# Keeping one more chunk of the input on chip: parking it in PSUM, with the re-read order adapted

## The chip, the cores and the metric

The kernel runs on one core of a Trainium2 chip. The metric is the device time of one execution in microseconds. Times are quoted as medians of several runs, all of which agreed within about 0.6%; no run of this study was in a slow state. The span that a profile page gives is about 2 us shorter than the time of the run that it was taken from.

In the lines of the profile, PE is TensorE (PEld its weight loads), DVE is VectorE, ACT is ScalarE, POOL is GpSimd and SP is SyncE; a q behind the name (ACTq, SPq) marks work of that engine's queue, here the issue of DMA transfers. SBUF is the on-chip memory that holds this kernel's buffers for chunks of the input, here called slots; PSUM is the on-chip memory into which its matmuls write their sums.

## The reference

A squeeze-and-excitation block. All of the input has to be seen before any of the output can be made:

```python
# x: (1, 256, 256, 384) bf16, w_down: (384, 24), w_up: (24, 384)
def reference(x, w_down, w_up):
    s = x.mean(axis=(1, 2))                       # over all 65,536 pixels
    s = _sigmoid(_silu(s @ w_down) @ w_up)        # 384 gates
    return x * s[:, None, None, :]
```

The input is 50.33 MB and so is the output. At least 100.66 MB must be moved; what is not kept on chip between the mean and the multiply is read a second time.

## The kernel before

The pixels are spread over 128 partitions, 512 rows of 384 channels in each. Sixteen rows make a chunk (12,288 bytes per partition, 1.57 MB in all), so there are 32 chunks. SBUF holds 17 slots of that size. The first 15 chunks are streamed through slots only for their sums, the other 17 stay:

```python
    JS = min(J, max(1, 12288 // (C * 2)))                    # 16 rows
    chunks = [(j0, min(JS, J - j0)) for j0 in range(0, J, JS)]
    NCH = len(chunks)                                        # 32
    ...
    n_slots = max(1, min(NCH, (avail - small_bytes) // bytes_per_slot))   # 17
    NS = NCH - n_slots                                       # 15 are read twice
    ...
    p1_order = [(stream_ids[k], k % n_slots) for k in range(NS)] + [
        (cache_ids[i], i) for i in range(n_slots)
    ]
    # load phase: for each chunk one DMA load; TensorE adds the rows up,
    # 16 matmuls with a column of ones per chunk, into one PSUM bank (sums_ps)
    ...
    # mean -> two tiny matmuls -> gate [128, 384] bf16
    ...
    for i in range(n_slots):                                 # kept chunks
        if i == 0:
            scale_and_store(i, cache_ids[i], piece_rows=[1, 3, 4, 8])
        elif i == 1:
            scale_and_store(i, cache_ids[i], piece_rows=[8, 8])
        else:
            scale_and_store(i, cache_ids[i])
    for k in range(NS):                                      # re-read chunks
        sl = k % n_slots
        j0, jsz = chunks[stream_ids[k]]
        nc.sync.dma_start(out=slots[sl][:, :jsz, :], in_=x3[:, j0:j0 + jsz, :])
        scale_and_store(sl, stream_ids[k])
```

`scale_and_store` multiplies in place on VectorE (`tensor_tensor`, slot times broadcast gate) and stores from the ScalarE queue. A reload of slot k must wait until the store out of slot k has landed. Both queues' transfers use eight completion semaphores in turn (in the trace, eight numbers that come back with every eighth load), so a transfer also waits for the one eight places before it.

## Time and profile before

| | before |
|---|---|
| time, median | 308.12 us (308.00 to 308.35, 12 runs) |
| span of the profile | 306.3 us |
| bytes moved | 124.38 MB: 32 + 15 chunks read, 32 written |
| busy: TensorE / VectorE | 30% / 35% |

Head of the page of the kernel before. The GB/s row has 40 equal slices of the span; the load phase is the left part, the store phase the right one.

```profile
span 306.3 us, 1307 instructions
PE 91.1 (30%) x519; PEld 43.9 (14%) x519; DVE 106.6 (35%) x40; ACT 2.1 (1%) x4; POOL 2.5 (1%) x8
...
GB/s 294 423 424 427 422 428 425 426 424 428 424 424 427 425 428 335 50 337 390 430 428 427 430 435 428 427 426 437 430 425 428 437 427 428 428 437 425 430 428 287
DMA packets 12518, 124.38 MB, mean 406 GB/s; under 512 B 1492, under 2 KB 1632, under 8 KB 2784
...
HBM read 73.96 MB, written 50.33 MB: 406 GB/s over the span
```

No compute engine is near full. Apart from both ends and a dip in the middle, every slice stands at 422 to 437 GB/s. The windows view of the same kernel puts numbers to the stretches. Its columns are: from and to, length, then busy us (and instructions) of each engine, then the granted TensorE clock, the busy share of the DMA engines (a packet is counted whole in the stretch in which it starts, so the share can come out a little above 1), and GB/s.

```profile
4.00:119.00 115.00, 85.01 (x480) 40.81 (x480) 0.00 (x0) 0.00 (x0) 0.00 (x0) 1.00 1.01 424
119.00:131.00 12.00, 6.13 (x39) 3.02 (x38) 4.51 (x7) 0.65 (x2) 0.00 (x0) 0.89 0.35 133
131.00:143.00 12.00, 0.00 (x0) 0.00 (x0) 12.00 (x6) 0.00 (x0) 0.00 (x0) 0.50 0.97 351
143.00:302.00 159.00, 0.00 (x0) 0.00 (x0) 90.03 (x28) 0.00 (x0) 0.00 (x0) 0.50 1.01 430
```

In two stretches, 274 us together, the DMA share is 1.01 and the rate 424 to 430 GB/s: a byte less there is time less. Two lines of the timeline of the store phase (start, length, what, count, idle before) tell how far the stores run behind VectorE:

```profile
127.93 148.52 ACTq L217 DMA_DIRECT2D out_dram<-slot  x36
...
250.87 3.36 DVE L211 TENSOR_TENSOR slot<-slot,gate 128x6144 bf16<-128x6144 bf16 x1 [3.98 <-DMA slot<-in_x_dram]
```

The last multiply ends at 254.2 us, but the span ends at 306.3: 52 us of stores are queued behind it. This suggests that VectorE could be late in the store phase at no cost.

### The profile page before, as it was taken

What the parts mean: (1) busy time and instruction counts of PE and PEld (TensorE: products, weight loads), DVE (VectorE), ACT (ScalarE), POOL (GpSimd) and SP (SyncE); (2) the same over time, 40 slices, a digit from 0 to 9 for tenths busy, and PEclk for the clock granted to TensorE, in tenths of its full rate; (3) what the DMA queues carried; (4) which work ended last, traced back from release to release, by engine and by line L of the source; (5) the groups of instructions that cost most, each with busy time, mean ns of one, the idle gap of its engine ahead of it and who ended that gap; (6) DMA issues with size and microseconds to landing.
All of it is one profiled execution on the core that took longest, in us unless ns stands there. A gap on an engine that the chain in (4) does not pass through costs nothing.

```text
span 306.3 us, 1307 instructions
## 1 busy us (share of the span) xinstructions
PE 91.1 (30%) x519; PEld 43.9 (14%) x519; DVE 106.6 (35%) x40; ACT 2.1 (1%) x4; POOL 2.5 (1%) x8
## 2 busy tenths in 40 slices
PE   0977677777777777300000000000000000000000
PEld 0433233333333333100000000000000000000000
DVE  0000000000000000499999999998444442000000
ACT  1000000000000000000000000000000000000000
POOL 3000000000000000000000000000000000000000
PEclk9999999999999999855555555555555555555555
DMA  7999999999999998199999999999999999999996
GB/s 294 423 424 427 422 428 425 426 424 428 424 424 427 425 428 335 50 337 390 430 428 427 430 435 428 427 426 437 430 425 428 437 427 428 428 437 425 430 428 287
DMA packets 12518, 124.38 MB, mean 406 GB/s; under 512 B 1492, under 2 KB 1632, under 8 KB 2784
## 3 DMA queue, kind: packets, MB, share of 16 engines
q1 hardware_dynamic: 7200, 73.93, 57.7%
q10 hardware_dynamic: 5184, 50.33, 38.8%
q8 instruction: 4, 0.07, 0.1%
q0 software_dynamic: 128, 0.04, 0.1%
q14 instruction: 2, 0.02, 0.0%
HBM read 73.96 MB, written 50.33 MB: 406 GB/s over the span
## 4 chain that ended last, share of the span: by engine, by line
DMA 70%; DVE 7%; issue 2%; PE 2%; SPq 1%; ACT 0%; DVEq 0%; ACTq 0%
DMA slot<-in_x_dram 43%; DMA out_dram<-slot 28%; DVE slot L211 7%; PE sums_ps L111 2%; SPq L104 1%; DVE mean_bf L133 0%; ACT gate L189 0%; DVE z1bc L171 0%; PE zz_ps L182 0%; PE meanT_ps L143 0%; PE z_ps L161 0%; DVE meanT_sb L152 0%; ACT s L169 0%; DVEq L211 0%; SPq L231 0%
## 5 line engine op out<-in xcount | busy, mean ns | idle before, releaser
L211 DVE TENSOR_TENSOR slot<-slot,gate 128x6144 bf16<-128x6144 bf16 (+4 forms) x36 | 105.5, 2994 | 22.1 <-DMA slot<-in_x_dram 21.2
L111 PE MATMUL sums_ps<-slot,ones_bf 128*1 128x384 bf16 x512 | 90.4, 332 | 34.3 <-DMA slot<-in_x_dram 34.3
L111 PEld LDWEIGHTS <-ones_bf 128*1 128x1 bf16 x512 | 43.5, 85 | 80.8 <-issue 43.2
L133 DVE TENSOR_SCALAR mean_bf<-sums_ps 1x384 bf16<-1x384 f32 x1 | 0.5, 546 | 123.9 <-PE sums_ps L111 123.9
L127 POOL DMA_DIRECT2D wd_sb<-in_w_down_dram x3 | 1.8, 604 | 0.8 <-POOLq L247 0.8
L81 ACT ACT_TABLE_LOAD x1 | 1.3, 1283 | 0.7 <-PEq L247 0.7
L169 ACT ACTIVATE s<-z_ps 24x1 f32<-24x1 f32 x1 | 0.2, 160 | 123.8 <-PE z_ps L161 123.8
L129 POOL DMA_DIRECT2D wu_sb<-in_w_up_dram x1 | 0.5, 539 | 0.0
L182 PE MATMUL zz_ps<-wu_sb,z1bc 24*128 24x384 bf16 x1 | 0.3, 331 | 0.6 <-DVE z1bc L171 0.6
L171 DVE TENSOR_SCALAR z1bc<-z_ps,s 24x128 bf16<-24x128 f32 x1 | 0.3, 339 | 0.5 <-ACT s L169 0.5
L189 ACT ACTIVATE gate<-zz_ps 128x384 bf16<-128x384 f32 x1 | 0.5, 491 | 0.8 <-PE zz_ps L182 0.8
L143 PE MATMUL meanT_ps<-ones_bf,mean_bf 1*128 1x1 bf16 x3 | 0.2, 163 | 0.6 <-DVE mean_bf L133 0.6
L78 DVE MEMSET ones_bf<- 128x8 bf16 x1 | 0.1, 65 | 0.8 <-PEq L247 0.8
L161 PE MATMUL z_ps<-meanT_sb,wd_sb 128*24 128x1 bf16 x3 | 0.2, 163 | 0.3 <-DVE meanT_sb L152 0.3
L143 PEld LDWEIGHTS <-mean_bf 1*128 1x128 bf16 x3 | 0.1, 91 | 1.0 <-DVE mean_bf L133 1.0
L152 DVE CAST meanT_sb<-meanT_ps 128x3 bf16<-128x3 f32 x1 | 0.2, 163 | 0.3 <-PE meanT_ps L143 0.3
L161 PEld LDWEIGHTS <-wd_sb 128*24 128x24 bf16 x3 | 0.2, 89 | 0.3 <-issue 0.2
L81 ACT ACTIVATE dummy<-ones_bf 1x1 f32<-1x1 bf16 x1 | 0.2, 202 | 0.0
L182 PEld LDWEIGHTS <-z1bc 24*128 24x128 bf16 x1 | 0.1, 90 | 0.7 <-DVE z1bc L171 0.7
L247 POOL MEMSET const-bfloat16-1.0<- 128x1 bf16 x1 | 0.1, 102 | 0.0
L247 POOL MEMSET const-float32-0.0<- 128x1 f32 x1 | 0.1, 99 | 0.2 <-issue 0.2
L247 POOL MEMSET const-float32-1.0<- 128x1 f32 x1 | 0.1, 99 | 0.0
(1 smaller groups left out, 0.1 us busy)
## 6 DMA issues: line engine op xcount, KB each, us to landing
slot<-in_x_dram SPq DMA_DIRECT2D x46, 1536.0 KB, 29.4
out_dram<-slot ACTq DMA_DIRECT2D x30, 1536.0 KB, 29.2
out_dram<-slot ACTq DMA_DIRECT2D x3, 768.0 KB, 3.8
slot<-in_x_dram SPq DMA_DIRECT2D x4, 384.0 KB, 22.8
out_dram<-slot ACTq DMA_DIRECT2D x1, 384.0 KB, 2.3
out_dram<-slot ACTq DMA_DIRECT2D x1, 288.0 KB, 2.1
out_dram<-slot ACTq DMA_DIRECT2D x1, 96.0 KB, 1.7
wd_sb<-in_w_down_dram POOLq DMA_DIRECT2D x3, 6.0 KB, 5.9
```

The costliest lines, as they stand in the source:

```text
L81: nc.scalar.activation(out=dummy[:1, :1], in_=ones_bf[0:1, 0:1], func=ACT.Sigmoid)
L104: nc.sync.dma_start(out=st[:, r0:r0 + rsz, :], in_=x3[:, j0 + r0:j0 + r0 + rsz, :])
L111: nc.tensor.matmul(sums_ps[ci][:1, :csz], ones_bf[:, 0:1], st[:, jj, c0:c0 + csz], start=first, stop=last,)
L127: nc.gpsimd.dma_start(out=wd_sb[:csz, kt, :], in_=w_down[c0:c0 + csz, :])
L129: nc.gpsimd.dma_start(out=wu_sb[:R, :], in_=w_up[:, :])
L133: nc.vector.tensor_scalar(out=mean_bf[:1, c0:c0 + csz], in0=sums_ps[ci][:1, :csz], scalar1=1.0 / float(N), scalar2=None, op0=ALU.mult,)
L143: nc.tensor.matmul(meanT_ps[:csz, kt:kt + 1], mean_bf[0:1, c0:c0 + csz], ones_bf[0:1, 0:1], start=True, stop=True,)
L161: nc.tensor.matmul(z1_ps[:R, 0:1], wd_sb[:csz, kt, :], meanT_sb[:csz, kt:kt + 1], start=(kt == 0), stop=(kt == KT - 1),)
L182: nc.tensor.matmul(zz_ps[:, :csz], z1bc[:R, :], wu_sb[:R, c0:c0 + csz], start=True, stop=True,)
L189: nc.scalar.activation(out=gate[:, c0:c0 + csz], in_=zz_ps[:, :csz], func=ACT.Sigmoid)
L211: nc.vector.tensor_tensor(out=st[:, r0:r0 + rsz, :], in0=st[:, r0:r0 + rsz, :], in1=gate_b, op=ALU.mult,)
L247: nc = _bacc.Bacc("TRN2", target_bir_lowering=False, num_devices=1)
```

## The change

By the constants that the program reads when it is built (`PSUM_NUM_BANKS`, `PSUM_BANK_SIZE_BYTES`), PSUM has eight banks of 2 KB per partition, and the kernel needs two at a time. The change takes the other six, exactly 12,288 bytes per partition (the tile `xps`, 128x3072 fp32), to keep one more chunk. All of the kernel's big loads and stores go to and from slots in SBUF, so VectorE copies the chunk in (as fp32 words) while its sum is taken, and later multiplies straight out of PSUM into a slot that is stored. Slot 1 serves as that staging slot, so its own reload is moved to the end. The small PSUM tiles now share banks.

```diff
+    psum_misc_banks = len(cn_chunks) + 1
+    ...
+        spare = ((psum_banks_total - psum_misc_banks) * nc.PSUM_BANK_SIZE_BYTES) // (C * 2)
+        psum_rows = max(0, min(spare, JS, J - cached_rows))          # 16
+    streamed_rows = J - cached_rows - psum_rows                      # 14 chunks
 ...
-        psum.tile([1, csz], FP32, name=f"sums_ps_{i}")
+        psum.tile([1, csz], FP32, name=f"sums_ps_{i}", tag=f"wide{i}")
+        xps = psum.tile([P, psum_rows, C // 2], FP32, name="xps")
 ...
+        def park(st):
+            nc.vector.tensor_copy(out=xps[:, :, :], in_=st[:, :pjsz, :].bitcast(FP32))
+        read_and_reduce(pj0, pjsz, psl, after=park)
 ...
-    meanT_ps = psum.tile([P, KT], FP32)
+    meanT_ps = psum.tile([P, KT], FP32, tag="narrow")
 ...  (z1_ps: tag "narrow"; zz_ps: tag "wide")
+                in0=src[:, r0:r0 + rsz, :] if src is not xps else src[:, r0:r0 + rsz, :].bitcast(BF16),
 ...
+    if psum_chunk is not None:
+        pj0, pjsz = psum_chunk
+        stage_sl = 1 if n_slots > 1 else 0
+        stage = slots[stage_sl]
+        scale_and_store(xps, stage, pj0, pjsz)
-    for k in range(NS):
-        sl = k % n_slots
-        j0, jsz = chunks[stream_ids[k]]
-        nc.sync.dma_start(out=slots[sl][:, :jsz, :], in_=x3[:, j0:j0 + jsz, :])
-        scale_and_store(sl, stream_ids[k])
+    for k in [0] + list(range(2, NS)) + [1]:
+        j0, jsz = stream_chunks[k]
+        st = slots[k % n_slots]
+        nc.sync.dma_start(out=st[:, :jsz, :], in_=x3[:, j0:j0 + jsz, :])
+        scale_and_store(st, st, j0, jsz)
```

(Cut: the bookkeeping of chunk lists and the split of the load helper, which leave the work as it is.)

More of the change, by code (lines that the diff above doesn't have):

```diff
@@ L42 @@
     JS = min(J, max(1, 12288 // (C * 2)))
-    chunks = [(j0, min(JS, J - j0)) for j0 in range(0, J, JS)]
-    NCH = len(chunks)
     bytes_per_slot = _pad32(JS * C * 2)
@@ L58 @@
     avail = nc.sbuf_top - nc.sbuf_base
-    n_slots = max(1, min(NCH, (avail - small_bytes) // bytes_per_slot))
-    NS = NCH - n_slots
-    stream_ids = list(range(NS))
-    cache_ids = list(range(NS, NCH))
+    n_slots = max(1, min((J + JS - 1) // JS, (avail - small_bytes) // bytes_per_slot))
+    cached_rows = min(J, n_slots * JS)
+    psum_banks_total = nc.PSUM_NUM_BANKS
+    psum_misc_banks = len(cn_chunks) + 1
+    psum_rows = 0
+    if J > cached_rows and psum_misc_banks < psum_banks_total:
+        spare = ((psum_banks_total - psum_misc_banks) * nc.PSUM_BANK_SIZE_BYTES) // (C * 2)
+        psum_rows = max(0, min(spare, JS, J - cached_rows))
+    streamed_rows = J - cached_rows - psum_rows
+    stream_chunks = []
+    j0 = 0
+    rem = streamed_rows % JS
+    if rem:
+        stream_chunks.append((j0, rem))
+        j0 += rem
+    while j0 < streamed_rows:
+        stream_chunks.append((j0, JS))
+        j0 += JS
+    NS = len(stream_chunks)
+    psum_chunk = (streamed_rows, psum_rows) if psum_rows > 0 else None
+    cache_chunks = []
+    j0 = streamed_rows + psum_rows
+    while j0 < J:
+        rows = min(JS, J - j0)
+        cache_chunks.append((j0, rows))
+        j0 += rows
+    assert len(cache_chunks) == n_slots or J <= cached_rows
+    n_slots = len(cache_chunks)
     x3 = x.flatten_outer_dims().rearrange("(p j) c -> p j c", p=P)
@@ L83, with reduce_rows, read_and_reduce @@
     sums_ps = [
-        psum.tile([1, csz], FP32, name=f"sums_ps_{i}")
+        psum.tile([1, csz], FP32, name=f"sums_ps_{i}", tag=f"wide{i}")
         for i, (c0, csz) in enumerate(cn_chunks)
     ]
-    p1_order = [(stream_ids[k], k % n_slots) for k in range(NS)] + [
-        (cache_ids[i], i) for i in range(n_slots)
-    ]
+    xps = None
+    if psum_chunk is not None:
+        xps = psum.tile([P, psum_rows, C // 2], FP32, name="xps")
     total_mm = J
     mm_state = {"idx": 0}
-    def read_and_reduce(ch, sl, pieces):
-        j0, jsz = chunks[ch]
+    def reduce_rows(st, r0, rsz):
+        for jj in range(r0, r0 + rsz):
+            first = mm_state["idx"] == 0
+            last = mm_state["idx"] == total_mm - 1
+            for ci, (c0, csz) in enumerate(cn_chunks):
+                nc.tensor.matmul(
+                    sums_ps[ci][:1, :csz],
+                    ones_bf[:, 0:1],
+                    st[:, jj, c0:c0 + csz],
+                    start=first,
+                    stop=last,
+                )
+            mm_state["idx"] += 1
+    def read_and_reduce(j0, jsz, sl, pieces=1, after=None):
         st = slots[sl]
@@ L106, in read_and_reduce @@
             )
-            for jj in range(r0, r0 + rsz):
-                first = mm_state["idx"] == 0
-                last = mm_state["idx"] == total_mm - 1
-                for ci, (c0, csz) in enumerate(cn_chunks):
-                    nc.tensor.matmul(
-                        sums_ps[ci][:1, :csz],
-                        ones_bf[:, 0:1],
-                        st[:, jj, c0:c0 + csz],
-                        start=first,
-                        stop=last,
-                    )
-                mm_state["idx"] += 1
-    for n, (ch, sl) in enumerate(p1_order):
-        remaining = len(p1_order) - n
-        pieces = 4 if remaining == 1 else 1
-        read_and_reduce(ch, sl, pieces)
+            reduce_rows(st, r0, rsz)
+        if after is not None:
+            after(st)
+    for k, (j0, jsz) in enumerate(stream_chunks):
+        read_and_reduce(j0, jsz, k % n_slots)
+    if psum_chunk is not None:
+        pj0, pjsz = psum_chunk
+        psl = NS % n_slots
+        def park(st):
+            nc.vector.tensor_copy(out=xps[:, :, :], in_=st[:, :pjsz, :].bitcast(FP32))
+        read_and_reduce(pj0, pjsz, psl, after=park)
+    for i, (j0, jsz) in enumerate(cache_chunks):
+        pieces = 4 if (i == n_slots - 1 and jsz >= 4) else 1
+        read_and_reduce(j0, jsz, i, pieces=pieces)
     wd_sb = consts.tile([P, KT, R], BF16)
@@ L157 @@
             )
-    z1_ps = psum.tile([R, 1], FP32)
+    z1_ps = psum.tile([R, 1], FP32, tag="narrow")
     for kt, (c0, csz) in enumerate(ck_chunks):
@@ L180 @@
     for ci, (c0, csz) in enumerate(cn_chunks):
-        zz_ps = psum.tile([P, csz], FP32, name=f"zz_ps_{ci}")
+        zz_ps = psum.tile([P, csz], FP32, name=f"zz_ps_{ci}", tag=f"wide{ci}")
         nc.tensor.matmul(
@@ L191, with scale_and_store @@
         )
-    def scale_and_store(sl, ch, piece_rows=None):
-        j0, jsz = chunks[ch]
-        st = slots[sl]
+    def scale_and_store(src, dst, j0, jsz, piece_rows=None):
         if piece_rows is None:
@@ L211, in scale_and_store @@
             nc.vector.tensor_tensor(
-                out=st[:, r0:r0 + rsz, :],
-                in0=st[:, r0:r0 + rsz, :],
+                out=dst[:, r0:r0 + rsz, :],
+                in0=src[:, r0:r0 + rsz, :] if src is not xps else src[:, r0:r0 + rsz, :].bitcast(BF16),
                 in1=gate_b,
@@ L217, in scale_and_store @@
             nc.scalar.dma_start(
-                out=out3[:, j0 + r0:j0 + r0 + rsz, :], in_=st[:, r0:r0 + rsz, :]
+                out=out3[:, j0 + r0:j0 + r0 + rsz, :], in_=dst[:, r0:r0 + rsz, :]
             )
-    for i in range(n_slots):
+    for i, (j0, jsz) in enumerate(cache_chunks):
+        st = slots[i]
         if i == 0:
-            scale_and_store(i, cache_ids[i], piece_rows=[1, 3, 4, 8])
+            scale_and_store(st, st, j0, jsz, piece_rows=[1, 3, 4, 8])
         elif i == 1:
-            scale_and_store(i, cache_ids[i], piece_rows=[8, 8])
+            scale_and_store(st, st, j0, jsz, piece_rows=[8, 8])
         else:
-            scale_and_store(i, cache_ids[i])
-    for k in range(NS):
-        sl = k % n_slots
-        j0, jsz = chunks[stream_ids[k]]
-        nc.sync.dma_start(out=slots[sl][:, :jsz, :], in_=x3[:, j0:j0 + jsz, :])
-        scale_and_store(sl, stream_ids[k])
+            scale_and_store(st, st, j0, jsz)
+    if psum_chunk is not None:
+        pj0, pjsz = psum_chunk
+        stage_sl = 1 if n_slots > 1 else 0
[5 more added lines that the diff above has]
+        nc.sync.dma_start(out=st[:, :jsz, :], in_=x3[:, j0:j0 + jsz, :])
+        scale_and_store(st, st, j0, jsz)
 _INS = ['x', 'w_down', 'w_up']
```

## The prediction

> **What bounds the kernel now.** Bytes moved by DMA. The page of the kernel before shows 124.38 MB in a span of 306.3 us, mean 406 GB/s; the chain that ended last is 70% DMA (loads into slots 43%, stores 28%). By the windows view, 4 to 119 us (loads and sums) runs at 424 GB/s with DMA share 1.01, and 143 to 302 us (scale, store, reload) at 430 GB/s, share 1.01. No engine competes: PE is busy 30%, DVE 35%. Only three stretches are not at full rate: the start, 119 to 131 us (last sums, gate, first store: 133 GB/s) and 131 to 143 us (small pieces: 351 GB/s). The Trainium skill, "DMA: Bandwidth & Descriptors", Specifications, gives a fabric ceiling of 435 GB/s; the trace agrees (428 to 437 in full slices), although the 358 GB/s per core listed beside it is exceeded. So the rate cannot rise; only bytes or the slow stretches can shrink.
>
> **What the change does.** Before, 17 of 32 chunks stay in slots and 15 are read twice. The change parks one 16-row chunk in six PSUM banks, so 14 are read twice.
> - Removed: one reload of 1.57 MB, 1 of 79 chunk transfers (1.26% of all bytes). At 430 GB/s that is 3.66 us. It is in the saturated part, hence on the critical path.
> - Added: one DVE copy, slot to PSUM (128x3072 fp32), about 3.3 us as an estimate from the 3.35 us of a 128x6144 bf16 multiply at two elements per cycle. It falls into the load phase, where DVE is idle for 123.9 us (waits view); the slot it reads is loaded again 15 chunks later. Cost: nothing.
> - Changed: one of the 128x6144 multiplies reads PSUM. "VectorE: DVE Perf Modes", the perf-mode tier table, puts tensor_tensor with a PSUM operand at 1x; scaled from the 3.35 us seen, I estimate 6.3 us. No trace shows it yet. DVE is then several chunks ahead of the stores (it produces a chunk per 3.3 us, and with reloads interleaved a store lands only every 7.3 us), so the extra 3 us is hidden.
> - Moved: the reload of slot 1 now comes last, behind the store of the parked chunk, the 18th. I expect it issued near 250 us and landed near 258 to 262 us. Stores are then queued for 40 us more (before, the last multiply ends at 254 us and stores drain to 304 us), so the late load is covered.
> - The second reload starts one store later (about 147 instead of 143.7 us); stores alone fill DMA there, as DVE feeds 480 GB/s.
> - Shared PSUM banks for the small tiles follow orders that already exist: nothing.
>
> **Predicted time:** 308.12 - 3.7 = 304.4 us, range 303.6 to 305.8. Faster by over 2%: 0.02; within 2%: 0.96; slower by over 2%: 0.02.
>
> **What would show it.** Bytes fall to 122.8 MB and HBM reads to 72.4 MB; the GB/s row stays at 424 to 437 until the end; load phase and gate end within 0.5 us of before (gate at 127.5 us); the copy appears near 60 us in the load phase, with no PE or queue wait behind it; the PSUM multiply takes 5.5 to 7 us and no store queue runs dry after it; the span shortens by 3.3 to 3.9 us, all after 150 us.
>
> **What would make it wrong.** A hole in the GB/s row after 200 us, because stores share completion lanes with loads and one waits for the late reload (then less is gained); a slower mixed rate around 131 to 150 us because the loads are offset by one; the DVE copy holding up the loads; or the last reload arriving so late that its multiply and store stick out at the end.

## The result, and the profile after

The changed kernel took 304.59 us (304.32 to 304.71, 8 runs), against 308.12 us before. The ratio is 0.9884, 95% interval 0.9874 to 0.9894. (Ratios here are the mean time of one kernel's runs over that of the other's in the same rounds, so they are not quite the ratios of the medians.) It is 3.5 us or 1.2% faster, which is within 2% as forecast.

The head of the page of the changed kernel, the same lines as before:

```profile
span 302.6 us, 1303 instructions
PE 92.3 (30%) x519; PEld 44.2 (15%) x519; DVE 109.9 (36%) x41; ACT 2.1 (1%) x4; POOL 2.5 (1%) x8
...
GB/s 298 420 422 428 422 426 430 421 432 417 429 426 421 435 419 401 19 323 352 440 417 442 421 437 422 435 429 427 439 419 440 419 440 422 435 424 434 430 427 291
DMA packets 12374, 122.81 MB, mean 406 GB/s; under 512 B 1476, under 2 KB 1616, under 8 KB 2768
...
HBM read 72.39 MB, written 50.33 MB: 406 GB/s over the span
```

Bytes fell by 1.57 MB and the mean rate stayed at 406 GB/s. The span fell by 3.7 us, and 1.57 MB at 430 GB/s is 3.65 us. The windows view of the changed kernel shows where:

```profile
4.00:119.00 115.00, 86.13 (x480) 41.11 (x480) 3.36 (x1) 0.00 (x0) 0.00 (x0) 0.99 1.01 424
119.00:131.00 12.00, 6.13 (x39) 3.03 (x38) 4.46 (x7) 0.65 (x2) 0.00 (x0) 0.84 0.34 131
131.00:143.00 12.00, 0.00 (x0) 0.00 (x0) 12.00 (x6) 0.00 (x0) 0.00 (x0) 0.50 0.96 348
143.00:298.30 155.30, 0.00 (x0) 0.00 (x0) 89.99 (x28) 0.00 (x0) 0.00 (x0) 0.50 1.01 430
```

The first three stretches stand nearly as they did (424, 131 and 348 GB/s, against 424, 133 and 351). The last one runs at the same 430 GB/s but is shorter: the whole gain lies after 143 us. The groups of instructions by line that the change touched (busy us, mean ns; idle before and its releaser):

```profile
L154 DVE COPY xps<-slot 128x3072 f32<-128x3072 f32 x1 | 3.4, 3361 | 59.3 <-DMA slot<-in_x_dram 59.3
...
L245 DVE TENSOR_TENSOR slot<-xps,gate 128x6144 bf16<-128x6144 bf16 x1 | 3.3, 3348 | 0.0
```

The copy into PSUM came after 59.3 us of idleness of VectorE, in the load phase. The multiply out of PSUM took 3348 ns. That is the time of the same multiply out of SBUF (3351 ns mean of 29 in this profile), not the 6.3 us that had been estimated. From the timeline of the store phase:

```profile
127.97 144.73 ACTq L251 DMA_DIRECT2D out_dram<-slot  x36
...
246.72 0.33 SPq L271 DMA_DIRECT2D slot<-in_x_dram  x1
...
258.36 3.36 DVE L245 TENSOR_TENSOR slot<-slot,gate 128x6144 bf16<-128x6144 bf16 x1 [15.16 <-DMA slot<-in_x_dram]
```

The late reload was issued at 246.72 us. VectorE waited 15.16 us for it, yet nothing came of that: the stores were issued until 272.7 us (127.97 + 144.73), and the DMA rate has no hole.

### The profile page after: what moved, and what is told of

The parts are those of the page before. It is cut to its first block, busy times and chain, and to the rows that moved or that the text cites. A ratio compares the mean times of both kernels' runs of the same rounds, so it can differ in the third digit from the quotient of the medians.

```text
span 302.6 us, 1303 instructions
## 1 busy us (share of the span) xinstructions
PE 92.3 (30%) x519; PEld 44.2 (15%) x519; DVE 109.9 (36%) x41; ACT 2.1 (1%) x4; POOL 2.5 (1%) x8
## 2 busy tenths in 40 slices
DMA packets 12374, 122.81 MB, mean 406 GB/s; under 512 B 1476, under 2 KB 1616, under 8 KB 2768
## 3 DMA queue, kind: packets, MB, share of 16 engines
HBM read 72.39 MB, written 50.33 MB: 406 GB/s over the span
## 4 chain that ended last, share of the span: by engine, by line
DMA 73%; DVE 6%; issue 4%; PE 2%; SPq 1%; ACT 0%; ACTq 0%; DVEq 0%
DMA slot<-in_x_dram 47%; DMA out_dram<-slot 26%; DVE slot L245 6%; PE sums_ps L122 2%; SPq L140 1%; DVE mean_bf L169 0%; ACT gate L225 0%; ACTq L251 0%; DVE z1bc L207 0%; PE zz_ps L218 0%; PE meanT_ps L179 0%; PE z_ps L197 0%; DVE meanT_sb L188 0%; ACT s L205 0%; SPq L271 0%
## 5 line engine op out<-in xcount | busy, mean ns | idle before, releaser
L245 DVE TENSOR_TENSOR slot<-slot,gate 128x6144 bf16<-128x6144 bf16 (+4 forms) x35 | 102.2, 2986 | 29.7 <-DMA slot<-in_x_dram 28.7
L122 PE MATMUL sums_ps<-slot,ones_bf 128*1 128x384 bf16 x512 | 91.5, 334 | 33.2 <-DMA slot<-in_x_dram 33.2
L154 DVE COPY xps<-slot 128x3072 f32<-128x3072 f32 x1 | 3.4, 3361 | 59.3 <-DMA slot<-in_x_dram 59.3
L245 DVE TENSOR_TENSOR slot<-xps,gate 128x6144 bf16<-128x6144 bf16 x1 | 3.3, 3348 | 0.0
```

The costliest lines, as they stand in the source:

```text
L122: nc.tensor.matmul(sums_ps[ci][:1, :csz], ones_bf[:, 0:1], st[:, jj, c0:c0 + csz], start=first, stop=last,)
L154: nc.vector.tensor_copy(out=xps[:, :, :], in_=st[:, :pjsz, :].bitcast(FP32))
L245: nc.vector.tensor_tensor(out=dst[:, r0:r0 + rsz, :], in0=src[:, r0:r0 + rsz, :] if src is not xps else src[:, r0:r0 + rsz, :].bitcast(BF1 ...
```

## The experiments

Theory "bytes": the gain is one reload that is no longer made, at the rate of the saturated stretch, and nothing else in the change matters to the time. The main rival is "order": the change also moves the reload of slot 1 and shifts the others by one, so fewer loads may meet stores at an unfavourable time. A second rival says that VectorE paces the stores and the change was lucky not to hit it.

Two parts of the change can be done apart, which gives four combinations: neither (308.08 to 308.24 us in the jobs below), order alone, parking alone, both.

### Order alone

```diff
 # kernel before
-    for k in range(NS):
-        sl = k % n_slots
+    for k in [0] + list(range(2, NS)) + [1]:
+        sl = n_slots - 1 if k == 1 else k % n_slots
```

(The destination is changed as well because the program order alone does not decide when a load is issued: with the loop's order changed but chunk 1 still going into slot 1, the scheduler that orders the instructions when the program is built put its load back in second place. That version was built and not run.)

> The kernel before, no parking, with only the moved reload: the reload of the second streamed chunk is issued last and lands in the slot that is stored 17th. Theory 'bytes' (one reload of 1.57 MB less at 430 GB/s is the whole gain): bytes stay at 124.38 MB, so 308.1 us, within 0.4. Rival 'order' (the gain comes from fewer and later loads mixing with the stores): 304.6 to 306 us.

Measured: 307.95 us, ratio 0.9995 (0.9983 to 1.0008). Moving the reload alone is worth nothing that these runs can tell: by the interval, between 0.5 us faster and 0.2 us slower.

### Parking alone

```diff
 # changed kernel
-        stage_sl = 1 if n_slots > 1 else 0
-        stage = slots[stage_sl]
-        scale_and_store(xps, stage, pj0, pjsz)
-    for k in [0] + list(range(2, NS)) + [1]:
+        stage = slots[NS]
+    for k in range(NS):
 ...
+    if psum_chunk is not None:
+        scale_and_store(xps, stage, pj0, pjsz)
```

> The changed kernel with parking kept and the order undone: reloads in natural order, the parked chunk multiplied and stored last of all, through slot 14, which is no longer needed then. Theory 'bytes': 122.81 MB, 304.6 us within 0.5. Rival 'order': back to 307 us or more.

Measured: 304.28 us, ratio 0.9878 (0.9864 to 0.9891), with 122.81 MB moved. The whole gain is there without the new order. The rival "order" falls on both runs.

### Half the dose

```diff
-        psum_rows = max(0, min(spare, JS, J - cached_rows))
+        psum_rows = max(0, min(spare, JS // 2, J - cached_rows))
```

> The changed kernel, parking 8 rows in place of 16, so half a chunk (0.79 MB) less is read. Theory 'bytes': half the gain, 308.12 - 1.8 = 306.3 us within 0.4. Rival 'order': the reload order is that of the changed kernel, so its full gain, about 304.6 us.

Measured: 306.17 us, ratio 0.9936 (0.9923 to 0.995), with 123.59 MB moved. Against the 308.08 us of the same job that is 1.9 us for 0.79 MB; 0.79 MB at 430 GB/s is 1.8 us. The gain goes with the bytes.

### More work for VectorE

```diff
         stage = slots[stage_sl]
+        half = C // 2
+        nc.vector.tensor_tensor(
+            out=stage[:, :, 0:half],
+            in0=xps[:, :, :],                                  # read as fp32
+            in1=gate[:, None, 0:half].to_broadcast([P, pjsz, half]),
+            op=ALU.mult,
+        )
+        nc.vector.tensor_copy(out=stage[:, :, :], in_=xps[:, :, :].bitcast(BF16))
         scale_and_store(xps, stage, pj0, pjsz)
```

The two results are overwritten by the proper one, so the output stays right.

> The changed kernel with two more VectorE instructions before the multiply of the parked chunk: one multiply that reads the parked chunk as 3072 fp32 per partition, one copy of it as 6144 bf16. Theory 'VectorE has slack there': no change, 304.6 us within 0.3, though VectorE is busy 6 to 10 us more. Rival 'VectorE paces the stores': the added busy time shows in the span, 308 us or more. On the cost itself: if PSUM operands drop multiplies to one element per cycle whatever their type, the 3072 fp32 multiply takes about 3.3 us and the 6144 bf16 one would take 6.3, against the 3.35 us seen; if only 4-byte elements do, the fp32 multiply takes 3.3 us and the bf16 one stays at 3.35.

Measured: 304.81 us, ratio 0.9894 (0.9881 to 0.9908). VectorE was busy 116.2 us instead of 109.9, and the time is 0.2 us above the 304.59 us of the changed kernel (which ran in another job), within what the intervals allow. What gave way is VectorE's waiting: its multiplies waited 22.4 us for reloads in this run, against 28.7 us in the changed kernel. So VectorE has slack for 6.3 us at this place; a cost of some tenths of a microsecond is not ruled out. The tile view of the parked chunk in this run (duration min/median/max in ns, first and last start, forms) gives the cost of each way to touch PSUM:

```profile
L154 DVE COPY xps<-slot x1: 3360/3360/3360, 60.1 to 60.1; 128x3072 f32<-128x3072 f32 x1
L268 DVE TENSOR_TENSOR slot<-xps,gate x1: 3347/3347/3347, 183.6 to 183.6; 128x3072 bf16<-128x3072 f32 x1
L274 DVE COPY slot<-xps x1: 3347/3347/3347, 190.2 to 190.2; 128x6144 bf16<-128x6144 bf16 x1
L245 DVE TENSOR_TENSOR slot<-xps,gate x1: 3347/3347/3347, 196.7 to 196.7; 128x6144 bf16<-128x6144 bf16 x1
```

All four take the same time, though two handle 3072 elements per partition and two handle 6144. Per element, 4-byte data in PSUM costs twice as much as 2-byte data here. For the bf16 multiply, PSUM costs nothing against SBUF (3347 against 3349 ns in this run), and that is where the estimate went wrong. For fp32 data and for the copies no run has the same work on SBUF alone, so what PSUM itself costs there is not shown.

### Can the slow stretch from 131 to 143 us be mended?

This looks for more, beyond the change. In that stretch the trace's packet records show the first reload's 128 packets of 12,288 bytes taking 613 ns on average (612 ns in the kernel before), where they take 460 ns later on. Two guesses were put to the test, in three runs.

First, slot 1 in one piece of 16 rows (`piece_rows=[16]` for `[8, 8]`):

> The changed kernel; slot 1 is multiplied and stored as one piece of 16 rows in place of two of 8. It asks what holds the stretch from 131 to 143 us at 348 GB/s, where load packets of 12288 bytes take longer (about 570 to 760 ns by the trace of before) than their usual 460 while store packets of 6144 bytes mix with them. Theory 'small store packets slow the mix': load packets go back to about 460 ns, the stretch gains 1 us, but up to 1 us is lost waiting for the larger multiply: 304.0 to 305.0 us. Rival 'first reload after the turn from reads to writes is slow': load packets stay at 560 ns or more.

Second, the changed kernel with the reloads in slots 2 to 15 in natural order, so that the first reload comes later:

```diff
-    for k in [0] + list(range(2, NS)) + [1]:
+    for k in range(NS):
         j0, jsz = stream_chunks[k]
-        st = slots[k % n_slots]
+        st = slots[k + 2]
```

> The changed kernel; the 14 reloads go in natural order into slots 2 to 15, so the first reload waits for the first store of a whole chunk and none meets the 8-row stores. Theory 'small store packets slow the mix': the stretch from 131 to 143 us rises from 348 to about 400 GB/s and the time falls by 0.5 to 1.5 us, to 303.1 to 304.1. Rival 'turn from reads to writes': the slow stretch moves later with the reload, and the time stays at 304.6.

Third, the same with slots 2 and 3 in halves as well (`elif i <= 3` for `elif i == 1`):

> As reload_from2, with slots 2 and 3 also multiplied and stored in halves, so that stores never wait for a whole multiply. If VectorE's 3.3 us per whole chunk leaves DMA short before the first reload, this is 0.3 to 0.8 us faster than reload_from2; if not, the same or slower by the smaller packets.

Measured: 305.29 us (ratio 0.9905, 0.9891 to 0.992), 305.42 us (0.9909, 0.9894 to 0.9924) and 304.72 us (0.9889, 0.9873 to 0.9906). The windows view from 131 us on, in steps of 6 us, of the changed kernel:

```profile
131.00:137.00 6.00, 0.00 (x0) 0.00 (x0) 6.00 (x4) 0.00 (x0) 0.00 (x0) 0.50 0.90 325
137.00:143.00 6.00, 0.00 (x0) 0.00 (x0) 6.00 (x3) 0.00 (x0) 0.00 (x0) 0.50 1.02 371
143.00:149.00 6.00, 0.00 (x0) 0.00 (x0) 6.00 (x3) 0.00 (x0) 0.00 (x0) 0.50 1.03 438
149.00:155.00 6.00, 0.00 (x0) 0.00 (x0) 6.00 (x3) 0.00 (x0) 0.00 (x0) 0.50 1.00 428
```

The same windows with slot 1 in one piece:

```profile
131.00:137.00 6.00, 0.00 (x0) 0.00 (x0) 6.00 (x3) 0.00 (x0) 0.00 (x0) 0.50 0.69 243
137.00:143.00 6.00, 0.00 (x0) 0.00 (x0) 6.00 (x3) 0.00 (x0) 0.00 (x0) 0.50 1.01 430
143.00:149.00 6.00, 0.00 (x0) 0.00 (x0) 6.00 (x3) 0.00 (x0) 0.00 (x0) 0.50 1.01 430
149.00:155.00 6.00, 0.00 (x0) 0.00 (x0) 6.00 (x3) 0.00 (x0) 0.00 (x0) 0.50 1.00 393
```

And with the reloads from slot 2 on:

```profile
131.00:137.00 6.00, 0.00 (x0) 0.00 (x0) 6.00 (x3) 0.00 (x0) 0.00 (x0) 0.50 0.90 369
137.00:143.00 6.00, 0.00 (x0) 0.00 (x0) 6.00 (x3) 0.00 (x0) 0.00 (x0) 0.50 0.86 359
143.00:149.00 6.00, 0.00 (x0) 0.00 (x0) 6.00 (x3) 0.00 (x0) 0.00 (x0) 0.50 1.08 344
149.00:155.00 6.00, 0.00 (x0) 0.00 (x0) 6.00 (x3) 0.00 (x0) 0.00 (x0) 0.50 0.95 397
```

In one piece, the first reload is soon fast (430 GB/s from 137 us on): apart from its first 29 packets (704 ns) its packets take 462 ns. But DMA is left waiting for the larger multiply (share 0.69), and a slow patch comes later: 393 GB/s from 149 to 155 us, where the stores' packets of 12,288 bytes take 509 ns on average. With the later first reload, the stores alone leave DMA short (share 0.86), and the slow stretch comes all the same, with the reload: 344 GB/s, its packets at 569 ns on average, though it now meets stores of whole chunks. So small store packets are not the whole cause.

The packet records allow a sum. Take the time that packets of 6,144 bytes and more took beyond 460 ns per 12,288 bytes, add it up from 128 to 165 us, and spread it over the 16 DMA engines: by this estimate the changed kernel loses 1.7 us, slot 1 in one piece 1.25 us, the reloads from slot 2 on 2.0 us, and the same with halves 2.2 us; the kernel before loses 1.7 us as well. After 165 us it is under 0.1 us in each of them. The loss comes once, near the first reloads, and these edits move it and change its size but none removes it. Whether the turn from reads to writes causes it is neither shown nor excluded; what slows the first reload is left open.

The first two runs lie outside what was expected of them (304.0 to 305.0 and 303.1 to 304.1 us) on the slow side; the rival's 304.6 us for the second was missed too. The third was met: halves in slots 2 and 3 win back 0.7 us over the plain late reload, and the total is that of the changed kernel. None of the piece sizes tried beats those in the kernel.

### Can the wait for the gate be shortened?

The stretch from 119 to 131 us, in which DMA mostly waits for the last sums and the gate, is the larger hole: at 131 in place of 430 GB/s it costs about 8 us, an estimate from the windows above, over twice what the change gained. In the changed kernel the last 32 matmuls of the sums run without a pause, as a line of its timeline shows (start, length, what, count, idle before):

```profile
119.38 5.36 PE L122 MATMUL sums_ps<-slot,ones_bf 128*1 128x384 bf16 x32 [0.94 <-DMA slot<-in_x_dram]
```

Sixteen of them can't start before a whole chunk has landed, so TensorE begins that backlog late. Loading the second last chunk in four pieces too should shrink it:

```diff
 # parked_last
-        pieces = 4 if (i == n_slots - 1 and jsz >= 4) else 1
+        pieces = 4 if (i >= n_slots - 2 and jsz >= 4) else 1
```

> parked_last with the last two chunks of the load phase, not the last one alone, loaded in four pieces. In the changed kernel 32 matmuls run back to back for 5.4 us after the last whole chunk lands, so the sums end later than their last rows land. With the second last chunk in pieces too, the sums should end about 0.9 us earlier, the gate also, and the whole kernel with it: about 303.5 us. If the sums' end is set by the last landing, no change: 304.3 us.

Measured: 303.62 us (303.37 to 304.2), ratio 0.9854 (0.9839 to 0.9869). The gate's activation started at 126.65 us instead of 127.06, so the gain in the chain was 0.4 us and not 0.9; and in the profiles of slot 1 in one piece and of the reloads from slot 2 on, whose load phase is that of the changed kernel and which ran in the same job as this run, it started at 127.00 and 126.82 us, so it may be 0.2 us. To see whether the time is real, the kernel was run again beside the changed kernel on one chip, with a version that loads the last chunk in eight pieces:

> The changed kernel itself, unedited, to stand beside the two below on one chip: 304.6 us within 0.2.

> tail_pieces unedited, on the same chip as the changed kernel. Its gate was ready 0.4 us earlier by the trace and its time 303.62 against 304.28 to 304.6 elsewhere. If that is real: 303.6 us, at least 0.6 below the changed kernel beside it, ratio intervals apart. If it was the chip: 304.3.

> tail_pieces with the last chunk in eight pieces of two rows. If the sums now wait for the last rows to land and then run them, fewer rows per piece save at most two matmuls, 0.3 us: 303.3 us. If issue or packets of 1536 bytes cost more, 303.6 us or more.

Measured: 304.40 us (304.18 to 304.47; ratio 0.9875, 0.9861 to 0.989) for the changed kernel, 303.78 us (303.29 to 305.03; 0.9863, 0.984 to 0.9886) for the pieces, and 304.22 us (304.04 to 304.44; 0.9869, 0.9852 to 0.9885) for the eight pieces. The medians of the pieces are 0.6 us better and the gate again stood earlier (126.53 against 126.88 us), but one of its four runs took 305.03 us and the intervals overlap. And the two kernels differ in more than the pieces: the version with pieces is built on parking alone, in natural order, which by itself measured 304.28 us, 0.3 us under the 304.59 us of the changed kernel; parking alone was not run in this job. So a gain from the pieces is possible and not shown. The eight pieces had the earliest gate of all (126.42 us) and no better time.

## Why the prediction was right

- **The sum.** Forecast 304.4 us, range 303.6 to 305.8; measured 304.59. The one term was 3.66 us for one reload at the rate of the saturated stretch. The span lost 3.7 us and the median 3.5 us, half the dose brought 1.9 us, and parking without the new order brought it all.
- **The ceiling.** The forecast took the DMA rate as fixed. The mean stayed at 406 GB/s and the long stretch at 430 GB/s. Single slices of the page spread to 417 to 442, wider than the forecast 424 to 437; that is a slip in reading how much one slice of 7.6 us scatters, without effect (in the kernel before, full slices already ran from 422 to 437).
- **Bytes.** 122.8 and 72.4 MB forecast, 122.81 and 72.39 MB read.
- **The copy in.** 3.3 us in idle time forecast; 3.36 us at 60.2 us, and nothing waited for it. The gate's activation ended at 127.55 us (127.51 before).
- **The multiply out of PSUM.** This step failed: 6.3 us estimated, with 5.5 to 7 us as the sign to look for, and 3.35 us measured. The estimate took the any-PSUM column of the table that it names and did not weigh the sentence below it on the same page. (Nor is 6.3 us what half the rate gives: multiplies of 3072 and 6144 elements take 1.75 and 3.35 us in the trace, so half the rate would be about 6.5 us, as an estimate.) It did not hurt the forecast because the term was argued to be hidden, and the experiment with 6.3 us of added VectorE work shows that it would have been.
- **The second reload.** Forecast for about 147 us, behind stores that fill DMA by themselves; it was issued at 147.19 us, and from 143.5 to 147.2 us DMA ran at share 1.00 and 428 GB/s.
- **The late reload.** Forecast as issued near 250 us and landed by 258 to 262 us; it was issued at 246.7 and its multiply started at 258.4 us, 14 us before the last store was issued.
- **What would make it wrong.** None came true: no hole in the rate after 200 us, hardly a slower mix (348 against 351 GB/s from 131 to 143 us), no held-up loads (424 GB/s in the load phase in both).

## What to carry to other kernels

When the DMA share stands at 1 over nearly the whole span, cost a change by its bytes alone, at the rate of the stretch in which they go away, and then check only whether what it adds has somewhere to hide; here 1.57 MB at 430 GB/s gave the answer within 0.2 us. Memory that lies idle can serve as cache, here PSUM, but the gain is bounded by its size: six banks hold one chunk out of the 15 that were read twice, so 1.2% is all there is. The copy in was free here because VectorE had nothing to do in the load phase, and added work in the store phase was free because stores were queued tens of microseconds behind VectorE; in a kernel that VectorE paces the same work should cost time, but no run here tests that.

## What the Trainium skill lacked or had wrong

- "VectorE: DVE Perf Modes", the perf-mode tier table, gives `tensor_tensor` with any PSUM operand 1x. The runs show 3.35 us for 128x6144 bf16 with one operand in PSUM, the same as from SBUF, and 3.35 us for half as many fp32 elements in PSUM. The section "Why PSUM operands drop a tier" on that page says at most 2x, and 1x for fp32; that sentence agrees with the runs, the table does not where the PSUM operand is bf16.
- The same table gives `tensor_copy` with PSUM at most 2x, without a type. Measured: 3.35 us for 6144 bf16 out of PSUM, 3.36 us for 3072 fp32 into PSUM, so in these two copies the 2-byte data went at twice the rate of the 4-byte data. The table is not wrong in this, and the section just named gives the type; the row lacks it.
- "DMA: Bandwidth & Descriptors", Specifications, lists 358 GB/s from HBM per core beside a fabric ceiling of 435 GB/s. With one core at work, 424 GB/s of loads and 430 GB/s of loads and stores mixed were seen for 115 and 155 us, so only the 435 is a useful bound here. The page isn't wrong about that everywhere: its Bandwidth section has 425 GB/s for one core and keeps the 358 for two cores that stream at once. The row lacks this condition.
- No page that was consulted explains why the first reload after the stores begin has 12,288-byte packets of 613 ns on average, against 460 ns later; the three runs above don't settle it either.
